# Filter groups of one batch each in a fused Fourier-filter and MLP-mixer kernel

## The chip, the cores and the metric

One core of one Trainium2 chip runs the whole program. The metric is the device time of one execution in microseconds, the median of the runs made. A separate, profiled execution supplies the trace. Engines are called as the profile calls them: PE is TensorE (PEld its weight loads), DVE is VectorE, ACT ScalarE, POOL GpSimd and SP SyncE, which issues most of the DMA transfers.

## The reference

All arrays are float32; x has 8 batches of 3008 tokens by 256 channels.

```python
X = np.fft.rfft(x, axis=1)                       # along the 3008 tokens
Y = X * (filt_r + 1j * filt_i)[None, :, :]       # 1505 frequencies x 256 channels
x = np.fft.irfft(Y, n=3008, axis=1)
h = np.maximum(x.transpose(0, 2, 1) @ w_tok1, 0.0) @ w_tok2     # 3008 -> 256 -> 3008
u = x + h.transpose(0, 2, 1)
out = u + np.maximum(u @ w_ch1, 0.0) @ w_ch2                    # 256 -> 1536 -> 256
```

## The kernel before, in words

**Two kinds of work share TensorE.** The *filter* (`dft`, L561) makes the Fourier transform, the product with the filter and most of the way back, for the batches of one group at a time (`GROUPS`, L56). The *mixer* (`mix`, L1132) does the two MLPs for one batch after another. The mixer is one long generator; after each piece of an item it yields a place, and the loop at L1319 decides there whether the next step of the filter of a coming group is issued. So the order of the work on every engine is written out by hand; nothing is scheduled later.

**The mixer's items.** A batch has six stretches of tokens, m = 0 to 5 (512 wide, the last 448), and each stretch six pairs of hidden blocks, jp = 0 to 5: 36 items a batch, numbered i within it. Products of matrices are done in seven parts by sums of operands in place of eight. In one item `up_first` makes four matmuls (L984), ACT copies one result away (L987), `up_middle` adds on VectorE (`hh<-ps_pg,s` and `s<-ps_pg,hh` at L962), `up_last` makes three matmuls (L1000) and its sums and ReLU, and `h_sums` and `down` work off the item before (L1018, seven matmuls). The places are 0 (behind the first part of `down`), 1 (behind `up_last`), 1.5 (behind the second part of `down`) and 2 (at the end). An fp32 matmul shows in the profile as two records, so L984 has eight records in an item. In each stretch `u_part` makes the operand of the next stretch: `u_quarter` in four parts for batches 1 to 7 (L905, L883), `u_unit` in two parts for batch 0 (L891, L883). `v_steps` and the six steps of `finish` (the residual sum and the transposes ahead of the output's stores) are VectorE work that `one_step` issues bit by bit. At item 32 (m = 5, jp = 2), place 2, `token_product` of the next batch runs: 12 rounds of 7 matmuls (L850), for which VectorE makes sums (`t4_sums`) and SP loads weights. The last six items of a batch are called its tail.

**The filter's steps.** Stage A is a transform of 64 points along one axis of the tokens, for a unit of 2 (untiled) or 4 (tiled) of its 24 columns. Stage B goes on along the other axis, multiplies with the filter and goes back, for 16 pairs of rows c. Between A and B, and behind B, the data goes through DRAM (`z_tmp`, `g_tmp`); the mixer loads the result as `t4`.
- Untiled stage A (`a_unit`, groups 0 and 1): 12 units a batch, each a full 128x128 matmul of 512 columns (L530), and a copy and a store (`z_out`).
- Tiled stage A (later groups): 6 units a batch. `x_sums` makes a sum and a difference of 512 columns on VectorE (L548, 0.68 us each), then `a_pair` makes four 64x64 matmuls on the four quarters of the array at once (L523). Such four are called a *set*. `leave` copies and stores.
- Stage B: `b_pair` is a set on what A left, `products` multiplies with the filter on VectorE (L705), `join` adds and subtracts (L710, L711), `bi_pair` is a set on the way back. In a group of two batches a set moves 512 columns, both batches beside each other, one c per step (`per = 1`). In a group of one batch `per = 2`: two c per step, two sets of 256 columns each for `b_pair` and for `bi_pair`.
- In tiled groups `bi_pair` of the step before follows directly on `b_pair`, so that one place on TensorE's order, here called a *slot*, has both. In group 1, which runs in batch 0, each has a place of its own.

**Where the groups stand.** Group 0 (batch 0) runs ahead of the mixer. Group 1 (batches 1 and 2) is issued within the mixer's batch 0, group 2 (3 and 4) in batches 1 and 2, group 3 (5 and 6) in batches 3 and 4, group 4 (batch 7) in batch 5; batches 6 and 7 carry none. A group must be done by item 32 of the last batch before its own; there the next group's generator starts and loads x. If it isn't, the build raises. Beside batch 0's first five items the last weights are converted as well (float64 bits to two float32 parts, on VectorE and ACT), and POOL makes the sums of w1, w2 and the channel weights in batch 0.

The table `due` (L1334 to L1343) names at which (jp, place) the coming step is issued. Its letters are the labels that `dft` yields: a (untiled unit), s (`x_sums`), d (two sets), c (`leave`), w (loads for B), b (`b_pair`), m (`join`), i (`bi_pair`).

Of the kernel before, what the change touches and what calls it, by code (L numbers as in the profile page):

```python
# [17 lines left out]
B = 8  # L18
# [37 lines left out]
GROUPS = ((0,), (1, 2), (3, 4), (5, 6), (7,))  # L56
# [71 lines left out]
def kernel(  # L128
# [432 lines left out]
    def dft(bs):  # L561
# [3 lines left out]
        per = 2 // nb if tiled else 1  # L565
# [40 lines left out]
        for i in range(0, len(todo) if tiled else 0, 2):  # L606
            if i + 2 == len(todo):
                zero_rows(0)
                w_load(0)
            sds = []  # L610
            for j in (i, i + 1):
                if j > i:
                    yield "s"
                sds.append(x_sums(*todo[j], j))
            yield "d"
            leave, leave_pg = [a_pair(*u, sd, tags) for u, sd, tags in zip(todo[i:i + 2], sds, (turn, ("pg", "pg")))]
            leave_pg()
            more(2)
            yield "c"
            leave()  # L620
            yield "s" if i + 2 < len(todo) else "w"
# [119 lines left out]
        if not first:  # L741
            last = K2 // KC
            for c in range(0, last, per):
                pss = b_pair(c)
                if c and tiled:
                    bi_pair(c - per, ("pg", "pg"))
                products(c, pss)
                for j in range(c + 2 * per, c + 3 * per):
                    if j < last:
                        t2_load(j)  # L750
                for j in range(c + min(2 * per, FB), c + min(2 * per, FB) + per):
                    if j < last:
                        w_load(j)
                yield "m"
                join(c)
                if not tiled or c + per == last:
                    yield "i"
                    bi_pair(c, turn)
                if c + per < last:
                    yield "b"  # L760
            return
# [79 lines left out]
    def token_product(b):  # L841
        one, two = (bank(tag).rearrange("p (s n) -> p s n", n=P) for tag in turn)
        for j in range(AP):
# [9 lines left out]
            if j + 2 < AP:  # L853
                t4_sums(b, j + 2)
        c = rp.tile([P, 8, P], FP32, tag="r", name="c")
# [276 lines left out]
    def mix(next_ready):  # L1132
# [11 lines left out]
        own = ({(4, 2): (0, 1)}, {(2, 2): (0,), (3, 0): (1,), (3, 2): (2, 3)})  # L1144
# [19 lines left out]
        for i in range(len(items) + 1):  # L1164
# [27 lines left out]
            if i < n:  # L1192
                one_step()
# [19 lines left out]
            if i >= n or i % n == n - 1:  # L1213
                one_step()
# [17 lines left out]
            if now:  # L1232
                if b + 1 < B and i % n == n - 4:
                    h1s[b + 1] = token_product(b + 1)
                u_parts(b, m, jp, 2)
                if jp == JP - 1:
                    while todo_v and m + 1 == MT:
                        one_step()
                if i >= 8 and to_dram:
                    to_dram.pop(0)()  # L1240
                if i in (28, 29):
                    w2m_load(i - 28)
# [5 lines left out]
    with tc.manual_schedule():  # L1248
# [70 lines left out]
        for b, i, place in mix(next_ready):  # L1319
# [10 lines left out]
            if done:  # L1330
# [4 lines left out]
            elif group:  # L1335
                tail = i >= n - JP
                sums_at = ((5, 1),) if tail else ((0, 1), (2, 1), (3, 1), (5, 1))
                due = (jp, place) in {"s": sums_at, "d": ((1, 1.5), (4, 1.5)), "c": ((2, 0), (5, 0)), "b": ((1, 1.5), (3 if tail else 4, 1.5)), "m": ((2, 2) if tail else (3, 1), (5, 1)),
                                      "i": ((0, 1.5), (3 if tail else 4, 1.5))}[coming]
            else:  # L1340
                due = (jp - (coming == "i")) % JP in ((5, 1, 2, 3) if i < 4 * JP else (5, 0, 1, 2, 3)) and place == {"b": 1, "m": 2, "i": 0}[coming]
            if coming == "a" and group == 0 and i < JP - 1:
                due = {0: 2, 1: 0, 1.5: 0, 2: 1}[place]  # L1343
# [34 lines left out]
```

## Time and profile before

| | |
|---|---|
| median of 3 runs | 2416.26 us (2415.17 to 2418.65) |
| profiled execution | 2418.01 us, span 2416.2 us |
| granted TensorE clock over the span | 0.996 |
| TensorE matmuls busy | 2374.1 us, 12340 records |
| VectorE busy | 1942.4 us |
| ScalarE, GpSimd busy | 690.5 us, 619.2 us |
| DMA | 278.65 MB, mean 115 GB/s |

How to read it: the span runs from the first to the last instruction of the program in the profiled execution, and that execution's own time is 1.8 us longer. "Busy" is the union of an engine's instructions. In a row of a group, the numbers behind the bar are busy time, mean duration of one, and idle time of the engine just before, with what ended it. In a row of a window they are listed in the order PE, PEld, DVE, ACT, POOL, then granted clock, DMA share and GB/s. The page's lines in 40 slices give the busy share in tenths.

### The profile page before, as it was taken

To read this page: it belongs to the slowest core of one execution; us is meant where nothing else is said; L and a number is where in the kernel's file an instruction comes from. 1 tells how busy PE (TensorE), PEld (TensorE's weight loads), DVE (VectorE), ACT (ScalarE), POOL (GpSimd) and SP (SyncE) were. 2 spreads that over 40 slices of the span, in tenths; PEclk is the share of its full clock that TensorE was granted. 3 is DMA by queue.
4 is the path that set the end of the run, shared out by engine and by line. 5 is a ranking of instruction groups with operands and counts; after the bars stand their busy time and mean duration, and the time that the engine had idled before them with its cause. 6 is when DMAs were issued, how large, how long until landed. Compare 5 with 4: busy or idle time off the path is not lost.

```text
span 2416.2 us, 35472 instructions
## 1 busy us (share of the span) xinstructions
PE 2374.1 (98%) x12340; PEld 1989.5 (82%) x12340; DVE 1942.4 (80%) x3673; ACT 690.5 (29%) x1339; POOL 619.2 (26%) x1115
## 2 busy tenths in 40 slices
PE   7989999999999999999999999999999999999998
PEld 4656676978888888988888888898888988898887
DVE  7798778777887888777788888877888777777776
ACT  5733322232222222123322222213222222222222
POOL 7476332113111211211121112112212112112121
PEclk8999999999999999999999999999999999999999
DMA  9985545534443223534344222344434111311100
GB/s 213 250 234 166 157 142 179 172 122 122 130 134 98 86 78 91 187 97 138 112 132 125 76 81 83 105 161 128 125 106 146 56 60 37 114 63 31 39 15 21
DMA packets 186011, 278.65 MB, mean 115 GB/s; under 512 B 35101, under 2 KB 122859, under 8 KB 185832
## 3 DMA queue, kind: packets, MB, share of 16 engines
q1 hardware_dynamic: 139544, 212.56, 28.7%
q0 software_dynamic: 34688, 53.83, 8.4%
q10 hardware_dynamic: 11600, 10.00, 1.4%
q8 instruction: 98, 1.61, 0.3%
q14 instruction: 81, 0.66, 0.1%
HBM read 193.52 MB, written 82.72 MB: 114 GB/s over the span
## 4 chain that ended last, share of the span: by engine, by line
PE 87%; DVE 6%; DMA 4%; issue 1%; POOL 1%; ACT 1%; SPq 0%; ACTq 0%; DVEq 0%; POOLq 0%
PE ps_po L1018 34%; PE ps_pg L984 19%; PE ps_pg L1000 14%; PE ps_b L523 4%; PE ps_b L850 3%; PE ps_acc L905 3%; PE ps_acc L850 2%; PE ps_b L905 2%; PE ps_pg L523 2%; PE ps_acc L883 2%; PE ps_b L883 2%; DMA st<-in_moe_w_tok_dram 1%; DVE t L962 1%; DVE hh L962 1%; DVE u L962 1%
## 5 line engine op out<-in xcount | busy, mean ns | idle before, releaser
L1026 POOL DMA_DIRECT2D out_dram<-r x752 | 407.9, 550 | 1611.9 <-issue 1149.2
L962 DVE TENSOR_TENSOR hh<-ps_pg,s 128x512 f32<-128x512 f32 (+3 forms) x864 | 482.4, 586 | 193.2 <-ACT s L987 191.3
L1005 ACT ACTIVATE hh<-hh 128x512 f32<-128x512 f32 (+1 forms) x576 | 347.8, 621 | 975.9 <-DVE hh L962 975.9
L1018 PE MATMUL ps_po<-t,wc 128*128 128x256 f32 (+1 forms) x2296 | 551.5, 379 | 1.8 <-DVE t L962 1.8
L1018 PEld LDWEIGHTS ps_po<-t,wc 128*128 128x128 f32 x2296 | 428.3, 190 | 110.2 <-issue 41.8
L984 PE MATMUL ps_pg<-v,wc 128*128 128x256 f32 (+1 forms) x1728 | 413.4, 376 | 1.7 <-POOL wc L381 1.6
L1018 PE MATMUL ps_po<-hh,wc 128*128 128x256 f32 (+1 forms) x1722 | 412.2, 375 | 0.6 <-POOL wc L382 0.6
L984 PEld LDWEIGHTS ps_pg<-v,wc 128*128 128x128 f32 x1728 | 327.9, 190 | 41.7 <-DVE v L962 3.2
L1018 PEld LDWEIGHTS ps_po<-hh,wc 128*128 128x128 f32 x1722 | 327.0, 190 | 39.4 <-POOL wc L382 1.7
L1000 PE MATMUL ps_pg<-u,wc 128*128 128x256 f32 (+1 forms) x1152 | 294.0, 378 | 1.9 <-DVE hh L962 1.3
L962 DVE TENSOR_TENSOR t<-t,hh 128x256 f32<-128x256 f32 (+1 forms) x576 | 246.2, 427 | 19.8
L1000 PEld LDWEIGHTS ps_pg<-u,wc 128*128 128x128 f32 x1152 | 216.3, 190 | 47.9 <-DVE hh L962 18.2
L962 DVE TENSOR_TENSOR s<-ps_pg,hh 128x512 f32<-128x512 f32 (+1 forms) x288 | 196.1, 681 | 30.7 <-DVE hh L962 0.9
L987 ACT COPY s<-ps_pg 128x256 f32<-128x256 f32 (+1 forms) x288 | 105.9, 368 | 343.6 <-PE ps_pg L984 339.3
L962 DVE TENSOR_TENSOR t<-hh 128x512 f32<-128x512 f32 (+1 forms) x288 | 195.4, 678 | 0.6 <-ACT hh L1005 0.6
L984 PE MATMUL ps_pg<-u,wc 128*128 128x256 f32 (+1 forms) x576 | 169.3, 376 | 2.4 <-DVE hh L962 2.4
L1000 PE MATMUL ps_pg<-v,wc 128*128 128x256 f32 (+1 forms) x576 | 168.9, 375 | 0.0
L984 PEld LDWEIGHTS ps_pg<-u,wc 128*128 128x128 f32 x576 | 108.3, 190 | 18.6 <-DVE hh L962 5.5
L1000 PEld LDWEIGHTS ps_pg<-v,wc 128*128 128x128 f32 x576 | 109.1, 190 | 12.7
L962 DVE TENSOR_TENSOR u<-ps_acc,u 128x256 f32<-128x256 f32 (+1 forms) x84 | 46.2, 550 | 80.4 <-PE ps_acc L905 56.9
L962 DVE TENSOR_TENSOR u<-ps_b,u 128x512 f32<-128x512 f32 (+2 forms) x126 | 74.5, 591 | 28.8 <-PE ps_b L905 26.7
L905 PE MATMUL ps_acc<-w 128*128 128x256 f32 (+1 forms) x336 | 85.3, 376 | 0.0
(164 smaller groups left out, 2638.6 us busy)
## 6 DMA issues: line engine op xcount, KB each, us to landing
w<-w_tmp SPq DMA_DIRECT2D x84, 448.0 KB
w<-w_tmp SPq DMA_DIRECT2D x35, 896.0 KB
out_dram<-r POOLq DMA_DIRECT2D x696, 32.0 KB, 2.2
g_tmp<-t SPq DMA_DIRECT2D x112, 192.0 KB
t<-g_tmp SPq DMA_DIRECT2D x42, 512.0 KB
t<-z_tmp SPq DMA_DIRECT2D x180, 96.0 KB
z_tmp<-t SPq DMA_DIRECT2D x60, 256.0 KB
filt<-in_x_dram SPq DMA_DIRECT2D x90, 128.0 KB
```

Source lines behind the costliest of these rows:

```text
L523: nc.tensor.matmul(outs(i, j), stat(i, j), mov(i, j), start=True, stop=True)
L850: nc.tensor.matmul(ps[:, at], w[:, n], mov, start=(j == 0 and i in (0, 2)), stop=(j == AP - 1 and i >= 5))
L883: nc.tensor.matmul(ps[:, ds(q * P, n)], t4[b, c][:, r, ts(dh, P)], wai[:, 0:n], start=(first and q == 0), stop=(not first and q == 3))
L905: nc.tensor.matmul(ps[:, ds(j * hw, hw)], h1[:, n, :], w2m[m % 2][:, at, 0:hw], start=(i < 2 and j == 0), stop=(j == len(todo) - 1))
L962: nc.vector.tensor_tensor(out=out, in0=in0, in1=in1, op=op)
L984: nc.tensor.matmul(ps[:, 0:hw], chan[0][:, jp, n, :], mov, start=True, stop=True)
L987: nc.scalar.copy(out=s[:, 0], in_=g[0][:, 0, 0:hw])
L1000: nc.tensor.matmul(ps[:, 0:hw], chan[0][:, jp, n, :], mov, start=True, stop=True)
L1005: nc.scalar.activation(out=hs, in_=hs, func=AF.Relu)
L1018: nc.tensor.matmul(po[i][:, j, 0:hw], chan[1][:, jp, n, :], mov, start=(jp == 0 and first == 1), stop=(jp == JP - 1 and last == 1))
L1026: q.dma_start(bass.AP(tensor=ob.tensor, offset=ob.offset + row * D + g * cw, ap=[[N1 * D, 32], [D if h else -D, n], [1, cw]]), blocks[ts(g ...
```

## The change

Each group now holds one batch, so there are eight groups, and batch b of the mixer carries the filter of batch b + 1, for b = 0 to 6. All groups but the first have `per = 2`: a slot of stage B has four sets of 256 columns in a row (two of `b_pair`, two of `bi_pair`), in batch 0 too. Group 1 (batch 1) keeps the untiled stage A, with half the units; batch 2 now goes through the tiled one.

The tiled stage A is laid out anew: a label e stands for one set alone. The first two units go as single sets in the tail of the batch before (jp 4 and 5), the other four as two double slots in m = 0. `x_sums` are issued one by one, and x is loaded one unit at a time behind each. The places of batch 0 become those of the other batches (stage B from item 6 on, two slots in each stretch), its untiled units come two per item instead of three, and its `u_unit` parts move to (3, 0) and (3, 2) from (4, 2). `token_product` becomes a generator that yields a place 1.7 in its tenth round, at which the table allows a `join` only. `one_step` is called in batch 0 where it is in the other batches.

```diff
-GROUPS = ((0,), (1, 2), (3, 4), (5, 6), (7,))
+GROUPS = tuple((b,) for b in range(B))
...
-        per = 2 // nb if tiled else 1
+        per = 1 if first else 2 // nb
...
-        for i in range(0, len(todo) if tiled else 0, 2):
-            if i + 2 == len(todo):
-                zero_rows(0)
-                w_load(0)
-            sds = []
-            for j in (i, i + 1):
-                if j > i:
-                    yield "s"
-                sds.append(x_sums(*todo[j], j))
-            yield "d"
-            leave, leave_pg = [a_pair(*u, sd, tags) for u, sd, tags in zip(todo[i:i + 2], sds, (turn, ("pg", "pg")))]
-            leave_pg()
-            more(2)
-            yield "c"
-            leave()
-            yield "s" if i + 2 < len(todo) else "w"
+        sums = []
+
+        def next_sum():
+            i = len(sums)
+            sums.append(x_sums(*todo[i], i))
+            more(1)
+
+        def sets(i, n):
+            return [a_pair(*u, sd, tags) for u, sd, tags in zip(todo[i:i + n], sums[i:], (turn, ("pg", "pg")))]
+
+        if tiled:
+            next_sum()
+            yield "s"
+            next_sum()
+            for i in range(2):
+                yield "e"
+                sets(i, 1)[0]()
+                yield "s"
+                next_sum()
+            for i in (2, 4):
+                yield "d"
+                leave, leave_pg = sets(i, 2)
+                leave_pg()
+                if i == 2:
+                    zero_rows(0)
+                    w_load(0)
+                yield "c"
+                leave()
+                for _ in range(2 * (i == 2)):
                     yield "s"
+                    next_sum()
+            yield "w"
...
-                if c and tiled:
+                if c:
                     bi_pair(c - per, ("pg", "pg"))
...
-                if not tiled or c + per == last:
+                if c + per == last:
                     yield "i"
                     bi_pair(c, turn)
...
             if j + 2 < AP:
                 t4_sums(b, j + 2)
+            if j + 3 == AP:
+                yield b - 1, MT * JP - 4, 1.7
...
-        own = ({(4, 2): (0, 1)}, {(2, 2): (0,), (3, 0): (1,), (3, 2): (2, 3)})
+        own = ({(3, 0): (0,), (3, 2): (1,)}, {(2, 2): (0,), (3, 0): (1,), (3, 2): (2, 3)})
...
-            if i < n:
+            if i < JP:
                 one_step()
...
-            if i >= n or i % n == n - 1:
+            if i >= JP:
                 one_step()
...
-                    h1s[b + 1] = token_product(b + 1)
+                    h1s[b + 1] = yield from token_product(b + 1)
...
-            if done:
+            if done or place == 1.7 and coming != "m":
                 continue
...
-            elif group:
+            else:
                 tail = i >= n - JP
-                sums_at = ((5, 1),) if tail else ((0, 1), (2, 1), (3, 1), (5, 1))
-                due = (jp, place) in {"s": sums_at, "d": ((1, 1.5), (4, 1.5)), "c": ((2, 0), (5, 0)), "b": ((1, 1.5), (3 if tail else 4, 1.5)), "m": ((2, 2) if tail else (3, 1), (5, 1)),
-                                      "i": ((0, 1.5), (3 if tail else 4, 1.5))}[coming]
-            else:
-                due = (jp - (coming == "i")) % JP in ((5, 1, 2, 3) if i < 4 * JP else (5, 0, 1, 2, 3)) and place == {"b": 1, "m": 2, "i": 0}[coming]
+                due = i >= JP * (group == 0) and (jp, place) in {
+                    "s": ((3, 1), (4, 1), (5, 1)) if tail else ((0, 1), (2, 1), (3, 1)),
+                    "e": ((4, 1.5), (5, 1.5)), "d": ((1, 1.5), (4, 1.5)), "c": ((2, 0), (5, 0)),
+                    "b": ((1, 1.5), (4, 1.5)), "m": ((2, 1.7) if tail else (3, 1), (5, 1)), "i": ((0, 1.5), (4, 1.5))}[coming]
             if coming == "a" and group == 0 and i < JP - 1:
-                due = {0: 2, 1: 0, 1.5: 0, 2: 1}[place]
+                due = place in (0, 2)
```

## Prediction

> **What bounds the kernel.** I read the page first (engines, clock, chain), then the windows of the eight batches, then TensorE's timeline item by item, then the windows of batch 0. From the page:
>
> ```profile
> PE 2374.1 (98%) x12340; PEld 1989.5 (82%) x12340; DVE 1942.4 (80%) x3673; ACT 690.5 (29%) x1339; POOL 619.2 (26%) x1115
> PEclk8999999999999999999999999999999999999999
> PE 87%; DVE 6%; DMA 4%; issue 1%; POOL 1%; ACT 1%; SPq 0%; ACTq 0%; DVEq 0%; POOLq 0%
> ```
>
> TensorE is busy 98% of the span at full granted clock, and 87% of the chain that ended last is its own. In the middle of the run a microsecond is won or lost only as TensorE work or as a gap in it. The windows below are cut at the first matmul (L984) of each batch:
>
> ```profile
> 139.40:476.60 337.20, 327.74 (x1614) 241.19 (x1613) 276.38 (x481) 99.99 (x191) 146.28 (x233) 1.00 0.57 173
> 476.60:764.60 288.00, 287.37 (x1541) 241.62 (x1540) 232.42 (x447) 80.10 (x158) 55.84 (x104) 1.00 0.40 125
> 764.60:1047.70 283.10, 283.10 (x1527) 242.00 (x1526) 235.72 (x443) 73.37 (x146) 54.38 (x101) 1.00 0.34 103
> 1047.70:1335.70 288.00, 287.36 (x1541) 241.60 (x1540) 232.41 (x447) 80.22 (x158) 55.80 (x104) 1.00 0.40 125
> 1335.70:1618.80 283.10, 283.10 (x1527) 241.98 (x1526) 235.69 (x443) 73.35 (x146) 54.37 (x101) 1.00 0.34 103
> 1618.80:1905.50 286.70, 285.96 (x1662) 246.11 (x1661) 234.72 (x461) 76.63 (x152) 55.92 (x104) 1.00 0.38 117
> 1905.50:2166.20 260.70, 260.70 (x1358) 237.09 (x1357) 199.22 (x401) 61.47 (x124) 54.36 (x101) 1.00 0.21 67
> ```
>
> After the bounds come the length and then the busy time of PE, PEld, DVE, ACT and POOL. Batch 6 carries no filter: 260.7 us is a bare batch. Batches 1 to 4 carry four filters for 27.3 + 22.4 + 27.3 + 22.4 us, batch 5 carries batch 7's alone for 26.0 us; together 125.4. Batch 0 carries two, beside the last weights, in 337.2 us. So the change takes one filter out of batch 0, gives one to batch 6, and recuts the ones between.
>
> **What a slot costs.** TensorE's timeline, an item with two sets of 512 columns and the bare item behind it, then one of batch 5 with four sets of 256:
>
> ```profile
> 1215.59 0.59 PE L984 MATMUL ps_pg<-u,wc 128*128 128x256 f32 x2
> ...
> 1221.77 1.04 PE L523 MATMUL ps_pg<-p,wb 64*64 64x512 f32 x8
> ...
> 1223.71 0.60 PE L984 MATMUL ps_pg<-u,wc 128*128 128x256 f32 x2
> ...
> 1229.75 0.60 PE L984 MATMUL ps_pg<-u,wc 128*128 128x256 f32 x2
> ```
> ```profile
> 1761.14 0.59 PE L984 MATMUL ps_pg<-u,wc 128*128 128x256 f32 x2
> ...
> 1767.33 1.04 PE L523 MATMUL ps_pg<-p,wb 64*64 64x256 f32 x16
> ...
> 1769.28 0.60 PE L984 MATMUL ps_pg<-u,wc 128*128 128x256 f32 x2
> ```
>
> From L984 to L984: 8.12 with the slot, 6.04 bare, so a slot of two 512 sets costs 2.08; four sets of 256 cost 8.14 - 6.04 = 2.10 (2.09 as a mean over batch 5). A slot with one 512 set or two 256 ones costs 1.22 (item of batch 1 at 620.1: 7.26). Hence 0.86 per 512 set and 0.36 per slot. The first slot of a batch's stage A (m0 jp1) costs more: 9.0 - 6.0 = 2.96, as the sums before it and the steps of `finish` push `up_middle` back on VectorE.
>
> [...]
>
> **Six tiled groups (batches 2 to 7), one batch each.** The places follow from the order of the yields and the `due` table.
> - Stage A: single sets in the last two items of the batch before (jp 4 and 5), at 1.22 each: 2.44. Then double ones at m0 jp1, with the sums at the same places as now: 2.96, and at jp4: 2.08.
> - Stage B: eight slots at jp1 and jp4 of m1 to m4. The first has only `b_pair`: 1.23. Seven with both: 7 x 2.09 = 14.63. The last `bi_pair` alone at m5 jp0: 6.89 - 5.67 = 1.22 by batch 2, plus 0.19 in the next item.
> - Sum 24.8 per group, 148.5 for six, against 125.4 now: **+23.1 us**.
>
> That counts the new `x_sums` in the tail at nothing. Each is two VectorE operations of 0.68. Their cover is VectorE's idle time there: in batch 2's tail it waits 1.27 and 1.55 us before `hh<-ps_pg,s` in the items at jp 4 and 5; the third sum lies where the present one does. 1.37 against 1.27 leaves about 0.1. Below, there is no gain to have from sums that are added. Above, the nearest row is the last `bi_pair` of batch 5, which in that tail cost 7.47 - 5.22 = 2.25 instead of 1.22 behind a joining of the same length: 1.0 per single set, 12 us over six tails. I take zero since the sums come after the operation that TensorE waits for next, while that joining came ahead of it.
>
> Edits with one answer. Products: four of 0.686 per slot in place of two of 1.217, 2.5 us more per batch on VectorE, which is at 235 of 283 us. Filter and table transfers for three more groups, on SP's queue ahead of w1, w2m and t4 loads: batch 5 issues exactly that many per batch at a DMA share of 0.38, without a gap in its slots of stage B. The t4 loads of a batch come in one go at the end, as they do in batches 2 and 4, whose token product takes 24.2 us as in batch 6. On SP's queue x units 3 to 5 and the z stores of the single sets now stand in the tail, ahead of the w2m load that m2 needs some nine items later. POOL's three clears of the filter rows (0.54 each) stand ahead of output stores that nobody waits for within a batch. The single sets' copies run on ACT, a quarter busy. In batch 0 the steps of `finish` move behind `up_last`, where later batches have them at bare items of 6.04. And the joining: the last one lies at m4 jp5, two items ahead of the token product, so at the new place nothing is waiting to be joined; that edit does nothing. Batch 5's late tail (7.47 above, and 24.46 for the product) goes for another reason, the earlier stage A, and is in the sum.
>
> **Batch 0, by rows of six items.** A full-array stage-A matmul is 0.85 us (two records). Windows of m0 and m2:
>
> ```profile
> 139.40:195.70 56.30, 49.79 (x182) 31.33 (x181) 50.46 (x89) 22.06 (x41) 45.39 (x75) 1.00 0.80 241
> 257.10:310.30 53.20, 52.48 (x257) 36.81 (x256) 44.34 (x74) 15.95 (x31) 18.78 (x31) 1.00 0.50 151
> ```
>
> - m0 (items 0 to 4 are the first row; 64.9 with item 5): VectorE, which still converts weights, is busy 50.5 of 56.3. Of 22 stage-A matmuls in batch 0 twelve go, five of them out of items 0 to 4; that frees TensorE, not VectorE. What helps is `u_unit`, 2.6 us each, now one at each of item 3's two places, not both at the end of item 4 (14.8 us). The sums of `v_steps` (1.5 us) move into this VectorE-bound stretch. I take 52 + 1.6 of waits for items 0 to 4 and 7.0 for item 5 (8.6 now): 60.5, or -4.5. Bounds: 0, if VectorE's queue stays as it is, and -9, by TensorE work alone.
> - m1 to m4 now: 52.8, 53.2, 52.2, 55.6. After: 6 x 6.04, two `u_unit` at 2.6, two slots of 2.09 = 45.7; m1 only 44.9, m4 0.4 less for its narrower `u`. I add 0.5 for waits (1.3 in m1, where POOL sums w1 and VectorE's 0.43 operations last 1.1): 46.2, 46.2, 46.2, 45.7, or -6.6, -7.0, -6.0, -9.9. Bounds: 1 us per row either way, the waits of now over the same count (52.2 - 51.2 in m3).
> - m5: `bi_pair` as in batch 2, 12.4 in place of 13.5: -1.1.
> - Sum **-35.1 us**.
>
> **Total.** 23.1 - 35.1 = -12.0. The profiled execution took 2418.0 (span 2416.2 and 1.8 around it), the median of the runs is 2416.3; 2416.3 - 12.0 = **2404**. One measurement can tell some 0.2% (4.8 us) from no change.
>
> **Rivals.**
> 1. The tail turns slower. Mechanism: VectorE's queue there. If x lands after the sum's place, or the sums run into `hh<-ps_pg,s`, `up_middle` waits and TensorE with it. For it: 1.37 us of work into 1.27 of idle time, twice in a row. Against: the first x transfer is issued at 1587.9 to 1590.9 in batch 4's tail, about 11 us ahead of the sum's place (1602.5). Price: the whole sums, 3 x 1.37 x 6 = 25 us, 2429. It decides from 16.8 / 6 = 2.8 us per tail on.
> 2. Batch 0 stays bound by VectorE and gives back little: m0 at 0 and 1 us less in each row, with 0.3 per tail: -2 to -5, 2411 to 2414. For it: 50.5 of 56.3 busy. Against: in m2 it is 44.3 of 53.2, and products and joins there fall from 15.3 to 8.3 us.
> 3. More is gained: the 0.88 us over a plain slot at m0 jp1 goes (6 x 0.88) and m0 saves 8: 2395.
> 4. That the change does not do what it says holds for the joining alone, as counted; if it did move, it would be a joining of 1.4 us beside the product's VectorE work, at most 1 us per tail.
>
> **Chances.** Forecast 0.64 (2398 to 2410), rival 1 0.10, rival 2 0.14, rival 3 0.12. Range 2396 to 2412: rival 1 and the far ends of 2 and 3 stay out. Faster by over 0.2% means below 2411.4: forecast, rival 3 and a third of rival 2, 0.80; within 0.2% 0.10; slower 0.10.
>
> **What would show it.** Batches 1 to 5 alike, each about 260.7 + 24.8 = 285.5 from L984 to L984; batch 6, without single sets in its tail, 283.1; batch 0 near 337.2 - 35.1 + 2.4 = 304.5, the 2.4 being the single sets in its tail, which the six groups' sum holds; batch 7 unchanged. Slots of m1 to m4 at 8.13. The tail's items at jp 4 and 5 1.2 us longer than now, 8.2 and 9.6. No joining (L710) between L850 records. Wrong if tail items grow by over 2 us, if items 0 to 4 of batch 0 stay at 56, or if slots of stage B show gaps.

## The result, and the profile after

The changed kernel takes 2410.6 us, the median of 9 runs (2407.8 to 2413.7); the kernel before took 2417.9 in the 9 runs beside them. The ratio is 0.9971, with a 95% interval of 0.9963 to 0.9979: 7.0 us less by the ratio (7.3 between the medians), where the prediction had 12.0. The profiled execution took 2411.5, with a span of 2409.7 against 2416.2. Line numbers below `zero_rows` (L588) moved down by 16 to 18: `up_first` is L1002 (was L984), `up_last` L1018 (was L1000), `down` L1036 (was L1018), VectorE's additions L980 (was L962), the joining L726, the products L721; `x_sums` stay at L548.

The page of the changed kernel, the same three lines:

```profile
PE 2363.4 (98%) x13132; PEld 2013.6 (84%) x13132; DVE 1954.8 (81%) x3781; ACT 689.2 (29%) x1339; POOL 629.8 (26%) x1124
PEclk8999999999999999999999999999999999999999
PE 91%; DVE 3%; DMA 2%; issue 1%; POOL 1%; ACT 1%; SPq 0%; DVEq 0%; ACTq 0%; POOLq 0%
```

TensorE has 792 more records in 10.7 us less busy time, and its share of the chain went from 87% to 91%, while VectorE's and the DMAs' shares were halved. The bound is the same. The clock's line in tenths shows nothing; the 6.8 us at half clock, shown below, are too short for a slice of 60 us. The windows of batches 0 to 6, cut at the weight load of their first L1002, 0.2 to 0.4 us ahead of the matmul itself (columns as before: length, PE, PEld, DVE, ACT, POOL, clock, DMA share, GB/s):

```profile
141.60:452.80 311.20, 296.81 (x1605) 240.79 (x1604) 253.50 (x472) 86.10 (x167) 147.28 (x233) 0.99 0.49 154
452.80:738.10 285.30, 285.29 (x1663) 245.98 (x1662) 234.83 (x461) 76.72 (x153) 56.78 (x104) 1.00 0.40 123
738.10:1022.90 284.80, 284.79 (x1662) 245.87 (x1661) 234.85 (x461) 76.68 (x153) 56.74 (x104) 1.00 0.40 124
...
1592.50:1877.50 285.00, 284.99 (x1661) 245.61 (x1660) 234.77 (x461) 76.38 (x153) 56.74 (x104) 1.00 0.40 123
1877.50:2159.90 282.40, 282.39 (x1646) 245.66 (x1646) 231.24 (x454) 74.84 (x149) 55.93 (x104) 1.00 0.36 112
```

Batches 1 to 5 are alike and filled to the last 0.01 us. The whole difference is found in four stretches of the span:

| stretch | before | forecast | after |
|---|---|---|---|
| start, up to batch 0 | 139.4 | 139.4 | 141.6 |
| batch 0 | 337.2 | 304.5 | 311.3 |
| batches 1 to 6 | 1689.6 | 1710.5 | 1707.0 |
| batch 7 | 250.1 | 250.1 | 249.8 |

The start has the same code in both kernels and took 137.8 to 142.2 in the twelve profiles of this study, so its 2.2 us lie within chance. Batches 1 to 6 cost 3.5 less than forecast. What is missing lies in batch 0, and there in one row of six items. Its m0, m1 and m2:

```profile
141.57:199.83 58.26, 50.20 (x200) 35.24 (x198) 55.04 (x99) 20.61 (x39) 46.56 (x76) 1.00 0.60 185
199.83:256.24 56.41, 50.09 (x243) 38.17 (x241) 42.44 (x66) 11.91 (x24) 35.55 (x48) 0.94 0.33 100
256.24:301.80 45.56, 45.56 (x257) 37.25 (x257) 36.73 (x69) 14.05 (x27) 18.43 (x31) 1.00 0.43 132
```

m2 is full and takes 45.6 (m3 and m4 45.7 each; forecast 46.2 and 45.7). m1 takes 56.4 where 46.2 was forecast: TensorE is idle for 6.3 of it, and the granted clock is 0.94. One item holds nearly all of that, item 7: 16.3 us. TensorE's timeline there, its releaser in brackets:

```profile
213.95 1.01 PE L523 MATMUL ps_acc<-t,wb 48*64 48x256 f32 x4
220.41 0.69 PE L523 MATMUL ps_b<-t,wb 48*64 48x256 f32 x2 [5.44 <-DMA t<-z_tmp]
```

The first slot of stage B has two sets of `b_pair`, each on a z unit of its own (the data that stage A left for one c). It ran the first and then stood 5.44 us for the second's z unit. The load was late because SP was late. SP's waits, its first instruction after the wait, and POOL's timeline at that time:

```profile
SPq L226 <- POOL filt L588: 40.4, 1, 40.4
```
```profile
206.53 0.31 SPq L226 DMA_DIRECT2D filt<-in_filt_r_dram  x1
...
209.77 0.30 SPq L667 DMA_DIRECT2D t<-z_tmp  x1
...
215.65 1.81 SPq L668 DMA_DIRECT2D t<-z_tmp  x4
```
```profile
199.26 6.78 POOL L829 TENSOR_TENSOR w<-w 128x384 f32<-128x384 f32 x6 [2.63 <-DMA w_tmp<-w]
205.98 1.45 POOL L588 MEMSET filt<- 128x512 f32 x3
207.40 11.13 POOL L829 TENSOR_TENSOR w<-w 128x384 f32<-128x384 f32 x10
```

Read from the bottom up: the three clears of the filter rows (`zero_rows`, L588) stand in POOL's queue behind six sums of w1 (L829). Those wait for the store of the raw w1 blocks and then take 6.8 us, so the first clear starts at 205.98. SP's queue holds the filter load, which overwrites the cleared tiles' other rows and waits for the clear, and behind it the z loads (L667, L668): those of the first unit from 209.77, then the next filter load, then those of the second unit from 215.65. The 40.4 us are SP's whole stand before that filter load, not a loss of that length. The clears need nothing of the sums; order alone puts them behind.

The kernel before had the same order, and its trace shows it too: POOL there runs all sixteen sums ahead of the clears, and the first set on a z unit comes 8.6 us after the first of them starts. POOL's timeline and TensorE's of the kernel before:

```profile
199.03 18.19 POOL L813 TENSOR_TENSOR w<-w 128x384 f32<-128x384 f32 x16 [4.27 <-DMA w_tmp<-w]
217.16 1.60 POOL L588 MEMSET filt<- 128x512 f32 x3
```
```profile
225.78 0.65 PE L523 MATMUL ps_b<-t,wb 48*64 48x512 f32 x2
...
234.73 0.65 PE L523 MATMUL ps_b<-t,wb 48*64 48x512 f32 x2
```

The change has the clears 11 us earlier and its first set 12.5 us earlier, at 213.24; that set still finds its z unit. But with `per = 2` the second set follows in the same slot, about 9 us after the clears start, where the kernel before has it in a later item, at 234.73, 17.6 us after them. So it is the second z unit that is no longer covered.

The idle time has a second price. The same row cut into stretches of 3.4 us, the seventh column the granted clock:

```profile
214.60:218.00 3.40, 0.37 (x2) 0.00 (x0) 3.40 (x5) 1.23 (x2) 3.16 (x4) 1.00 0.27 75
218.00:221.40 3.40, 0.99 (x8) 0.64 (x8) 1.08 (x1) 0.00 (x0) 0.53 (x1) 0.50 0.36 121
221.40:224.80 3.40, 3.40 (x13) 2.44 (x8) 2.48 (x4) 0.00 (x0) 0.00 (x0) 0.50 0.30 82
224.80:228.20 3.40, 3.40 (x17) 2.98 (x17) 2.23 (x5) 0.37 (x1) 0.00 (x0) 0.99 0.41 127
```

After a stretch in which TensorE was busy for 0.37 of 3.4 us the next one runs at half clock, and after one with 0.99 busy the next again. In the third stretch two records of L1002 take 1.06 us (223.69), at full clock 0.59 (556.99); by these rows I estimate half of 0.99 + 3.40, some 2.2 us more.

The tail of a batch answers the first rival. TensorE's timeline at the end of batch 2 (items of jp 4 and 5, each with a single set):

```profile
1013.49 0.54 PE L1002 MATMUL ps_pg<-u,wc 128*128 128x224 f32 x2
...
1021.20 0.65 PE L523 MATMUL ps_b<-sd,was 64*64 64x512 f32 x2
...
1023.08 0.59 PE L1002 MATMUL ps_pg<-u,wc 128*128 128x256 f32 x2
```

The item at jp 5 is 9.59 long, 8.38 before; that at jp 4 8.24, 7.02 before. Each is longer by 1.22, the bare price of a slot with one set, and VectorE still waits 1.58 us there after the new sum:

```profile
1012.02 1.28 DVE L548 TENSOR_TENSOR sd<-filt 128x512 f32<-128x512 f32 x2
1014.88 0.39 DVE L980 TENSOR_TENSOR hh<-ps_pg,s 128x224 f32<-128x224 f32 x1 [1.58 <-ACT s L1005]
```

### The profile page after: what moved, and what is told of

Same layout as the page of the kernel before. It is cut to its first block, busy times and chain, and to the rows that moved or that the text cites. A ratio compares the mean times of both kernels' runs of the same rounds, so it can differ in the third digit from the quotient of the medians.

```text
span 2409.7 us, 38162 instructions
## 1 busy us (share of the span) xinstructions
PE 2363.4 (98%) x13132; PEld 2013.6 (84%) x13132; DVE 1954.8 (81%) x3781; ACT 689.2 (29%) x1339; POOL 629.8 (26%) x1124
## 4 chain that ended last, share of the span: by engine, by line
PE 91%; DVE 3%; DMA 2%; issue 1%; POOL 1%; ACT 1%; SPq 0%; DVEq 0%; ACTq 0%; POOLq 0%
PE ps_po L1036 35%; PE ps_pg L1002 20%; PE ps_pg L1018 15%; PE ps_b L523 4%; PE ps_b L866 3%; PE ps_acc L923 3%; PE ps_acc L866 2%; PE ps_pg L523 2%; PE ps_b L923 2%; PE ps_b L901 2%; PE ps_acc L901 2%; DMA st<-in_moe_w_tok_dram 1%; DMA filt<-in_filt_r_dram 1%; DMA x<-in_x_dram 1%; DVE both L279 1%
## 5 line engine op out<-in xcount | busy, mean ns | idle before, releaser
L980 DVE TENSOR_TENSOR hh<-ps_pg,s 128x512 f32<-128x512 f32 (+3 forms) x864 | 481.4, 585 | 169.3 <-ACT s L1005 159.2
L1036 PE MATMUL ps_po<-t,wc 128*128 128x256 f32 (+1 forms) x2296 | 558.8, 380 | 0.5 <-DVE t L980 0.4
L1036 PEld LDWEIGHTS ps_po<-t,wc 128*128 128x128 f32 x2296 | 427.2, 190 | 96.4 <-issue 39.1
L1002 PE MATMUL ps_pg<-v,wc 128*128 128x256 f32 (+1 forms) x1728 | 412.7, 375 | 1.5 <-POOL wc L381 1.5
L1036 PE MATMUL ps_po<-hh,wc 128*128 128x256 f32 (+1 forms) x1722 | 411.5, 375 | 0.6 <-POOL wc L382 0.6
L1002 PEld LDWEIGHTS ps_pg<-v,wc 128*128 128x128 f32 x1728 | 328.2, 190 | 39.8 <-POOL wc L381 2.3
L1036 PEld LDWEIGHTS ps_po<-hh,wc 128*128 128x128 f32 x1722 | 326.8, 190 | 38.4 <-POOL wc L382 1.4
L1018 PE MATMUL ps_pg<-u,wc 128*128 128x256 f32 (+1 forms) x1152 | 291.9, 376 | 2.5 <-DVE hh L980 2.4
L980 DVE TENSOR_TENSOR t<-t,hh 128x256 f32<-128x256 f32 (+1 forms) x576 | 247.6, 430 | 19.8
L1018 PEld LDWEIGHTS ps_pg<-u,wc 128*128 128x128 f32 x1152 | 216.9, 190 | 34.1 <-DVE hh L980 8.0
L980 DVE TENSOR_TENSOR s<-ps_pg,hh 128x512 f32<-128x512 f32 (+1 forms) x288 | 196.0, 681 | 31.1 <-DVE hh L980 1.4
L980 DVE TENSOR_TENSOR t<-hh 128x512 f32<-128x512 f32 (+1 forms) x288 | 194.2, 674 | 0.6 <-ACT hh L1023 0.6
L1002 PE MATMUL ps_pg<-u,wc 128*128 128x256 f32 (+1 forms) x576 | 169.9, 377 | 3.9 <-DVE hh L980 3.9
L1018 PE MATMUL ps_pg<-v,wc 128*128 128x256 f32 (+1 forms) x576 | 168.8, 375 | 0.0
L1002 PEld LDWEIGHTS ps_pg<-u,wc 128*128 128x128 f32 x576 | 108.4, 191 | 20.1 <-DVE hh L980 7.8
L1018 PEld LDWEIGHTS ps_pg<-v,wc 128*128 128x128 f32 x576 | 108.9, 190 | 12.9
L980 DVE TENSOR_TENSOR u<-ps_acc,u 128x256 f32<-128x256 f32 (+1 forms) x84 | 46.1, 549 | 71.5 <-PE ps_acc L923 50.5
L980 DVE TENSOR_TENSOR u<-ps_b,u 128x512 f32<-128x512 f32 (+2 forms) x126 | 74.4, 591 | 28.9 <-PE ps_b L923 26.7
L721 DVE TENSOR_TENSOR p<-ps_b,filt 128x512 f32<-128x512 f32 x112 | 72.3, 685 | 16.2 <-PE ps_pg L523 13.4
```

The costliest lines, as they stand in the source:

```text
L721: nc.vector.tensor_tensor(out=prods[c, h][:, :, of(j)], in1=f, op=ALU.mult, in0=pss[h][:, of(j)].unsqueeze(1).to_broadcast([P, 2, nb, D]))
L980: nc.vector.tensor_tensor(out=out, in0=in0, in1=in1, op=op)
L1002: nc.tensor.matmul(ps[:, 0:hw], chan[0][:, jp, n, :], mov, start=True, stop=True)
L1018: nc.tensor.matmul(ps[:, 0:hw], chan[0][:, jp, n, :], mov, start=True, stop=True)
L1036: nc.tensor.matmul(po[i][:, j, 0:hw], chan[1][:, jp, n, :], mov, start=(jp == 0 and first == 1), stop=(jp == JP - 1 and last == 1))
```

## The experiments

Two questions were open: whether the wait in m1 comes from POOL's order, and what else of batch 0's rows each part of the change made. The table gives the rows of batch 0 in us (six items each; m5 takes 59.4 to 59.8 in all kernels of the changed layout), and the ratio to the kernel before. f2 and f4 are edits of the kernel before, all others of the changed one. The rows come from one profile each. e1 and e4 have the same code in batch 0, and their m1 takes 51.8 and 50.0; so a difference of that size in m1 is not told from chance. f3 leaves m0 and m1 as the changed kernel has them, and its item 7 takes 16.28 again.

| kernel | m0 | m1 | m2 | m3 | m4 | batch 0 | ratio (95%) |
|---|---|---|---|---|---|---|---|
| before | 64.9 | 52.8 | 53.2 | 52.2 | 55.6 | 337.2 | 1 |
| after | 58.3 | 56.4 | 45.6 | 45.7 | 45.7 | 311.3 | 0.9971 (0.9963 to 0.9979) |
| e1_early | 58.2 | 51.8 | 45.7 | 45.7 | 45.8 | 306.8 | 0.9954 (0.9939 to 0.9969) |
| e2_zero_dve | 59.5 | 48.4 | 45.7 | 45.7 | 45.8 | 304.7 | 0.9945 (0.9928 to 0.9961) |
| e3_early_u_late | 64.6 | 51.6 | 48.0 | 48.8 | 47.9 | 320.7 | 1.0003 (0.9994 to 1.0012) |
| e4_early_sum | 58.2 | 50.0 | 45.6 | 45.7 | 45.8 | 305.1 | 0.9963 (0.9948 to 0.9978) |
| f1_sums_later | 58.3 | 48.1 | 48.7 | 45.7 | 45.8 | 306.4 | 0.9948 (0.9935 to 0.9962) |
| f2_before_u_early | 67.1 | 54.9 | 53.1 | 53.1 | 55.8 | 341.6 | 1.0024 (1.0015 to 1.0034) |
| f3_tail_double | 58.1 | 56.2 | 45.7 | 45.7 | 45.8 | 310.9 | 0.9989 (0.9980 to 0.9998) |
| f4_before_sums_later | 64.9 | 56.4 | 53.9 | 52.2 | 55.2 | 341.0 | 1.0012 (1.0003 to 1.0021) |
| g1_sums_jp3 | 57.7 | 47.5 | 47.9 | 46.1 | 45.7 | 304.6 | 0.9949 (0.9935 to 0.9962) |
| g2_no_w1_sums | 58.1 | 45.2 | 45.7 | 45.7 | 45.7 | 299.9 | 2397.4 us, a single run |

**Group 1's last step, with the clears and loads, one item earlier** (`e1_early`):

```diff
-                due = place in (0, 2)
+                due = (place in (0, 2)) + ((i, place) == (JP - 2, 2))
```

> The step that clears the filter rows and issues batch 1's loads moves one item earlier, from item 5 (place 0) to the end of item 4, so that POOL gets the three clears ahead of the first six sums of w1. In the changed kernel item 7 of batch 0 takes 16.3 us, because the loads wait for the clears and these stand behind six sums that wait for a store. Theory (POOL's queue): the clears run at about 197 instead of 206, the loads follow, item 7 takes 7.3 to 8.5 us, and the whole is 8 to 9 us faster than the changed kernel, near 0.9936 of the kernel before (2402). Rival (the loads themselves, 27 transfers and the round trip through DRAM, are too slow for two items): item 7 stays over 13 us and the whole within 3 us of the changed kernel.

Medians 2406.9 against 2418.0. The z units are there in time (item 7 takes 7.9 in place of 16.3). POOL's timeline and the window of m1:

```profile
193.81 1.46 POOL L588 MEMSET filt<- 128x512 f32 x3
196.39 18.02 POOL L829 TENSOR_TENSOR w<-w 128x384 f32<-128x384 f32 x16 [1.11 <-DMA w_tmp<-w]
```
```profile
197.08:248.89 51.81, 48.41 (x241) 37.40 (x240) 41.06 (x66) 12.02 (x24) 34.16 (x45) 0.97 0.38 110
```

The clears now start 2.6 us ahead of the first sum, and 4.6 us of m1 come back; by the ratios the whole is about 4 us faster than the changed kernel, where 8 to 9 were expected. 6.6 above the row without the sums (45.2 in `g2_no_w1_sums`) stay: the wait for z is gone, but item 8 takes 10.89, with TensorE standing 2.66 us for VectorE at `up_last` and then 3.4 us at half clock. In e4's profile of the same code item 8 takes 9.43, and the clock is 1.00 from 205 to 232.

**The clears on VectorE** (`e2_zero_dve`):

```diff
-            nc.gpsimd.memset(filts[c][:, :, 0, :], 0.0)
+            (nc.vector if bs == GROUPS[1] else nc.gpsimd).memset(filts[c][:, :, 0, :], 0.0)
```

> Only the engine of the clears of group 1 changes, from POOL to VectorE; place and order of the loads stay as in the changed kernel. Theory (POOL's queue): the loads start when the last stage-A unit has left its buffer, near 196, and item 7 of batch 0 takes 7.5 to 9 us; item 5 grows by up to 1.5 us for three VectorE instructions; the whole is 6.5 to 8.5 us faster than the changed kernel. Rival (what the loads wait for is not the clears): item 7 stays at 16.

Medians 2403.2 against 2418.0. The clears leave POOL's queue and nothing else moves: m1 takes 48.4, 8.0 less, item 7 7.9. The window of m1, at full clock:

```profile
197.35:245.73 48.38, 46.12 (x239) 36.29 (x240) 39.71 (x66) 12.04 (x24) 32.31 (x44) 1.00 0.40 113
```

m0 pays 1.2 of it back (59.5), since VectorE, which sets the pace there, has the clears too (item 5: 7.44 in place of 5.97). e2 leaves the order of the loads alone, e1 leaves the engine alone, and both remove the wait; that it came from POOL's order is shown. By the ratios e2 is about 6 us faster than the changed kernel (6.5 to 8.5 expected).

**`u_unit` back at (4, 2)** (`e3_early_u_late`, on top of `e1_early`):

```diff
-        own = ({(3, 0): (0,), (3, 2): (1,)}, {(2, 2): (0,), (3, 0): (1,), (3, 2): (2, 3)})
+        own = ({(4, 2): (0, 1)}, {(2, 2): (0,), (3, 0): (1,), (3, 2): (2, 3)})
```

> As the kernel with the earlier loads, and the two u_unit parts of batch 0 go back to the end of jp 4, as before the change. Theory of the forecast: items 3 and 4 together grow by 2 to 3 us over the kernel with the earlier loads (in the changed kernel they take 13.2 + 9.0, before 10.4 + 14.8), since VectorE's conversions no longer lie under the first part; m1 to m4 stay within 0.3 us a row, where TensorE is the bound either way. Rival (the gain of m0 comes from the fewer stage-A matmuls): items 3 and 4 grow by less than 1 us.

Medians 2418.9 against 2418.0: all of the gain is gone, 12 us more than `e1_early`. m0 is back at 64.6 (before: 64.9), although five stage-A matmuls fewer lie in its first items: items 3 and 4 take 3.0 more than in `e1_early`, as the theory had it, and item 5, which it did not name, 3.5 more. And m2 to m4 take 2.1 to 3.1 us more, where 0.3 was expected: `u_unit` uses the banks of the slot just ahead. TensorE in m2, at jp 4:

```profile
290.58 1.13 PE L1036 MATMUL ps_po<-t,wc 128*128 128x256 f32 x4
293.37 1.95 PE L909 MATMUL ps_acc<-w,h 128*128 128x512 f32 x4 [1.66 <-DVE p L721]
```

The products (L721) of the slot at (4, 1.5) must have read `acc` before `u_unit` may write it. In the changed layout a slot lies at jp 4, so `u_unit` had to leave that place.

**The same move in the kernel before** (`f2_before_u_early`):

```diff
-        own = ({(4, 2): (0, 1)}, {(2, 2): (0,), (3, 0): (1,), (3, 2): (2, 3)})
+        own = ({(3, 0): (0,), (3, 2): (1,)}, {(2, 2): (0,), (3, 0): (1,), (3, 2): (2, 3)})
```

> The kernel before with one part of the change alone: batch 0's two u_unit parts at places (3, 0) and (3, 2). Theory (VectorE binds items 0 to 4, and the stand of u_unit matters elsewhere only where a slot's banks are in use): items 3 and 4 fall from 25.2 to about 22, m1 to m4 stay within 1 us a row; the whole is 1 to 4 us faster than the kernel before. Rival (moving u_unit frees TensorE in each row): all rows fall by 2 to 3 us, 10 us or more in the whole. Slower is possible too, if the steps at jp 3 then collide with the set at (3, 1): up to 2 us per row.

Medians 2424.2 against 2418.4: slower by 0.24%, where 1 to 4 us faster was expected. Items 3 and 4 fall from 25.2 to 22.8, near what was expected, but item 5 takes 13.8 in place of 8.6, and m0 67.1. There ACT stands 4.77 us in a copy of stage A for the store of an earlier one; the copy that `up_middle` needs is behind it in ACT's queue, TensorE then waits 3.24 us for `hh`, and the four records behind that wait take 1.63, where four of them take 1.03 in the kernel before (224.39):

```profile
198.41 0.58 ACT L539 COPY t<-ps_acc 128x512 f32<-128x512 f32 x1 [4.77 <-DMA z_tmp<-t]
200.32 1.63 PE L1000 MATMUL ps_pg<-u,wc 128*128 128x256 f32 x4 [3.24 <-DVE hh L962]
```

That alone is 5.2 us, more than batch 0 loses in all (4.5), so f2 does not price the move by itself. From m1 on the item at jp 3 takes 15.4, and the one at jp 4 gives most of that back (7.2, from 12.6). What e3 and f2 show is that here neither the new places without the move nor the move without the new places gained anything.

**The sums of w1 three items later** (`f1_sums_later`):

```diff
-            if JP - 2 <= i < JP + 2:
+            if i == JP - 2 or JP + 3 <= i < JP + 6:
```

> The changed kernel with POOL's sixteen sums of w1 issued in items 9 to 11 of batch 0 instead of items 5 to 7; nothing else moves. The clears of the filter rows then stand directly behind the channel weights' sums, and VectorE works beside an idle POOL in items 5 to 8. Theory (POOL does both harms in m1: its queue holds the loads back, and its own work slows VectorE's): item 6 6.1, item 7 7.3, item 8 6.1 to 7, items 9 to 11 up to 2 us more than in the changed kernel, m1 at 46 to 48 instead of 56.4, no half clock there; the whole 8 to 11 us faster than the changed kernel, near 0.993 of the kernel before. Rival (only the queue matters): as the kernel with the earlier loads, m1 at 51.8.

Medians 2407.1 against 2418.4; by the ratios between 5 and 6 us faster than the changed kernel, where 8 to 11 were expected. m1 comes out as the theory had it, not at the rival's 51.8. The wait goes here as well, by moving what stood ahead of the clears instead of the clears: item 7 takes 7.5. But the sums now slow items 10 to 13 (8.74, 8.42, 7.99, 9.25). Windows of m1 and m2:

```profile
199.86:248.01 48.15, 46.96 (x242) 36.62 (x240) 38.88 (x66) 12.01 (x24) 24.60 (x32) 1.00 0.33 94
248.01:296.73 48.72, 47.47 (x257) 36.82 (x257) 39.99 (x69) 13.93 (x27) 29.80 (x45) 1.00 0.47 148
```

**The same edit in the kernel before** (`f4_before_sums_later`):

> The kernel before with the sums of w1 in items 9 to 11, as a control: what the later sums bring without the change. There the loads of group 1 come two items later and the first set of stage B too, and items 5 to 8 are full of stage-A matmuls. Theory (the wait is made by the change): within 2 us of the kernel before. Rival (POOL's contention costs the kernel before as much): 5 us or more faster than it.

Medians 2421.2 against 2418.4: 2.8 slower, a little past the theory's 2, and nothing to be had; m1 rises by 3.6. In the kernel before, the late clears leave no wait that moving the sums could win back; the change took that cover away.

**The sums in two rounds of eight, at jp 3 of m1 and of m2** (`g1_sums_jp3`):

```diff
-            if JP - 2 <= i < JP + 2:
-                for _ in range(6 if i > JP - 2 else 1):
+            if i in (JP - 2, JP + 3, 2 * JP + 3):
+                for _ in range(8 if i > JP - 2 else 1):
...
-            elif i >= 2 * JP and i % 2 and w1_out:
+            elif i > 2 * JP + 3 and i % 2 and w1_out:
```

> The changed kernel with the sixteen sums of w1 in two lots of eight, in items 9 and 15 of batch 0, where u_unit gives TensorE 5.2 us more than VectorE's work there; the stores of the sums follow from item 17. Theory (the queue is free for the clears, and POOL's work lies where VectorE has room): items 5 to 8 as with the later sums (6.0, 6.0, 7.5, 6.0), items 10 to 13 lose most of the 5 us that the later sums cost there, m1 and m2 together 92 to 94 us (101.9 in the changed kernel, 96.8 with the sums in items 9 to 11); the whole near 2403 or below, 0.993 of the kernel before. Rival (VectorE is slowed wherever POOL works, and TensorE waits for it there too): m1 and m2 stay at 96 to 98.

Medians 2405.5 against 2417.4. m1 and m2 together take 95.4, f1's 96.9: between the theory's 92 to 94 and the rival's 96 to 98, and not clear of f1 by single profiles. Each round still costs: the items behind them take 8.74 and 7.81, then 8.79 and 7.54, where 8.03 and 6.04 are their lengths without sums.

**Without the sums** (`g2_no_w1_sums`):

```diff
-        for j in range(0, AP, 3):
+        for j in range(0, 0, 3):
```

> The changed kernel with the sixteen sums of w1 on POOL left out, so that the later token products work on unsummed weights. It bounds what POOL's work in m1 costs by queue and by contention together. Theory: the clears run at about 197, item 7 takes 7.3, m1 44.9 to 46 and m2 45.7, so 10.5 to 11.5 us less than in the changed kernel over the two rows. Rival (something else holds item 7): it stays over 12.

2397.4 in a single run. The windows of m0 and m1:

```profile
139.21:197.27 58.06, 51.45 (x200) 36.60 (x199) 54.85 (x99) 20.64 (x39) 47.18 (x78) 0.97 0.60 187
197.27:242.43 45.16, 45.16 (x241) 36.84 (x240) 35.76 (x67) 12.47 (x24) 16.30 (x27) 1.00 0.38 108
```

m1 is full, at 45.2: the prediction's count without waits was 44.9. So the forecast's items were sized rightly, and what m1 has above them goes with POOL's sums: first by their place ahead of the clears, as e1 and e2 show, and for the rest, by the rows on VectorE at the end of this document, by VectorE, which is slower beside them (2.24 us against 0.89 for two additions). In m0 the granted clock was 0.97, and the row is no longer for it: 58.06, against 58.26 at 1.00 in the changed kernel. TensorE does not set the pace there. m1 and m2 together take 90.8 here, and 94.0 to 97.5 with the sums in e1, e2, f1 and g1, wherever they stand.

**The first sum of m0 ahead of the first slot** (`e4_early_sum`, on top of `e1_early`):

```diff
-                    "s": ((3, 1), (4, 1), (5, 1)) if tail else ((0, 1), (2, 1), (3, 1)),
+                    "s": ((3, 1), (4, 1), (5, 1)) if tail else ((1, 0), (2, 1), (3, 1)),
```

> As the kernel with the earlier loads, and the fourth x_sums of each tiled group moves from item 0, place 1 to item 1, place 0, behind up_middle of item 1. In the changed kernel the slot of item 1 (m0 jp1) costs 2.64 us, 0.56 over a plain one. Theory (VectorE's order: these sums and the steps of finish push up_middle of item 1 back): the slot falls to 2.1 to 2.3, 0.3 to 0.5 us in each of six batches, 2 to 3 us in the whole. Rival (the finish steps alone hold VectorE, or the sums then come too late for the slot): no change, or worse by up to 0.7 us per batch.

Medians 2409.5 against 2418.0. The rival held: the item at m0 jp1 takes 9.15 in place of 8.65, in each of six batches: batches 1 to 6 rise from 1706.7 to 1709.6. (0, 1) is the better place of the two; why the first slot costs more than a plain one stays open.

**A double slot in the tail in place of two single ones** (`f3_tail_double`, its core):

```diff
-            for i in range(2):
-                yield "e"
-                sets(i, 1)[0]()
-                yield "s"
-                next_sum()
-            for i in (2, 4):
+            for i in (0, 2, 4):
...
-                for _ in range(2 * (i == 2)):
+                for _ in range(2 * (i < 4)):
...
-                    "s": ((3, 1), (4, 1), (5, 1)) if tail else ((0, 1), (2, 1), (3, 1)),
-                    "e": ((4, 1.5), (5, 1.5)), "d": ((1, 1.5), (4, 1.5)), "c": ((2, 0), (5, 0)),
+                    "s": ((3, 1), (4, 1)) if tail else ((0, 1), (0, 2), (2, 1), (3, 1)),
+                    "d": ((5, 1.5),) if tail else ((1, 1.5), (4, 1.5)), "c": ((0, 0), (2, 0), (5, 0)),
```

> The changed kernel with one double slot (jp 5, place 1.5) in the tail in place of two single sets; the third and fourth x_sums go to item 0, places 1 and 2. By the slot's fixed share of 0.36 us TensorE needs 0.36 less per batch, 2.2 us over six batches: the tail's items at jp 4 and 5 take 7.02 and 10.46 instead of 8.24 and 9.60. Against that VectorE has one more unit's sums (1.37 us) ahead of up_middle of item 1: theory (VectorE's queue decides at m0 jp1) the slot there rises from 2.64 to 3 to 4 us, and the whole is 0 to 6 us slower than the changed kernel. Rival (TensorE's work alone decides): 2 us faster.

Medians 2416.0 against 2418.4, by the ratios 4 to 5 us slower than the change, as the theory had it. The tail's two items do take less, 7.02 + 10.52 = 17.54 in place of 8.24 + 9.59 = 17.83: 0.29, near the 0.36 that a slot has fixed. But m0 now has the sums of two units ahead of its first slot, and there the first rival's mechanism works. VectorE and then TensorE in m0 of batch 3 (L975 and L1013 are L980 and L1018 of the changed kernel):

```profile
1029.70 1.28 DVE L548 TENSOR_TENSOR sd<-filt 128x512 f32<-128x512 f32 x2
1030.90 0.42 DVE L975 TENSOR_TENSOR hh<-ps_pg,s 128x256 f32<-128x256 f32 x1
```
```profile
1031.38 1.13 PE L1013 MATMUL ps_pg<-u,wc 128*128 128x256 f32 x4 [1.22 <-DVE hh L975]
```

`up_last` waits 1.22 us for an `hh` that stands behind the sum, and the item takes 9.87 in place of 8.66. With what the tail gains taken off, batches 1 to 6 are 5.5 us longer.

## Why the prediction was right, and what in it was wrong

The sign and the bound held: 2410.6 lies in the range of 2396 to 2412, near its upper end and 0.6 above the forecast's own 2398 to 2410. The mechanism held in the main: batch 0 gives 25.9, and batches 1 to 6 take 17.4 of it back. But that the time lies in the range is in part luck: the miss in m1 of batch 0 alone, 10.2 on 2404, would make 2414, outside it, and smaller errors the other way (steps 1, 5 and 7) brought it back. Step by step:

1. **Six tiled groups, +23.1.** Right in kind, 3.5 too high in batches 1 to 6. One full group costs 284.8 - 260.7 = 24.1, where 24.8 was forecast. Single sets in the tail 1.22 each, slots of stage B 8.13 - 6.04 = 2.09, the first 1.22, `bi_pair` at m5 jp0 1.22: as counted. The difference is m0: its first item takes 5.67, not 5.92, and the slot at jp1 costs 8.66 - 6.02 = 2.64, not 2.96.
2. **x_sums in the tail at nothing.** Right; the tail grew by the bare slots and by nothing else.
3. **Halved sets.** Right: the slots with four sets of 256 cost 2.09 in batches 1 to 6, where one with two sets of 512 costs 2.08 in the kernel before. So halving the sets costs about 0.01 us per slot here.
4. **The joining.** In batch 2 the last L726 is at 962.8, ahead of the token product at 975.6 to 999.8, and that item takes 24.22 as before. The edit does nothing, as counted.
5. **m0 of batch 0, -4.5.** It was -6.6, for the reason given: VectorE is busy 55.0 of 58.3, and e3 shows that the stage-A matmuls taken out, with all else that moved in m0, bring 0.3 without the move of `u_unit`. Items 0 to 4 take 52.3 (forecast 53.6), item 5 takes 5.97 (7.0).
6. **m1 of batch 0, -6.6.** This is the step that failed. It became +3.6: 10.2 us lie between forecast and result, twice the miss of the whole. When the z units of the first slot arrive is no term of the sum at all: their wait was put at nothing, without a reason. The one sentence on "POOL's three clears of the filter rows", which stand "ahead of output stores that nobody waits for", is among the tiled groups' edits, and it looked at what is behind the clears in POOL's queue. What is ahead of them decided in m1: six sums that wait for a store. And SP waits for the clears, with the z units that the slot needs behind that wait in its queue. And since `per = 2` asks for two units in one slot, the second came too late: TensorE stood 5.44 us, and the clock took an estimated 2.2 more. The rows of the kernel before that would have told it are shown above; I had read the length of the slots from the trace, but not when the operands of the first one come. The 1.3 that I had put into m1 for POOL's sums was the right suspect with a price for VectorE's slower operations alone.
7. **m2 to m5.** 45.6, 45.7, 45.7 against 46.2, 46.2, 45.7; there are no waits in them, and I had allowed 0.5. m5 has its 12.4 at jp 0 and 1.

Batch 0 came out 6.8 above the forecast: +10.2 in m1, -2.2 in m0, -1.2 in m2 to m4. With 3.5 less in batches 1 to 6, 2.2 of chance in the start and 0.3 less in batch 7, that takes the spans from the forecast's -11.8 to the -6.5 that was measured. The second rival named a time near the result (2411 to 2414), but not its cause: batch 0 gave the forecast's gain or more in every row but one, and that row was lost to a queue. Take the wait away, by e1, e2, f1 or g1, and batch 0 takes 304.6 to 306.8 (forecast 304.5), and the ratio is 0.9945 to 0.9954 (the forecast's 12.0 would be 0.9950). All four are faster than the kernel before. The intervals of e2, f1 and g1 lie just below that of the changed kernel, e1's overlaps it; among the four no order can be told. Without the sums of w1 (g2, a single run) batch 0 is another 4.7 to 6.9 us shorter; none of the places tried hides them.

What stays open: how much of the gain is the new cut of the groups and how much the new places in batch 0. e3 shows that the new places need `u_unit`'s move; the old stage-A layout with single-batch groups was not tried, since by the table its last set of stage B would come after the next group's start.

## What to carry to other kernels

When a step is moved, read each queue that it enters in both directions: what waits behind it, and what stands ahead of it and waits itself. Clears of 1.5 us on an engine that is busy for 26% of the span cost 8.0 us in m1 (by `e2_zero_dve`), because in POOL's queue they stood behind six sums that waited 2.63 us for another step's DMA and then took 6.78, and SP's queue passed that on to loads that had nothing to do with either. And a wait of TensorE in a full stretch can cost more than its length: here 5.44 us of idle time brought 6.8 us at half clock with them, by the estimate above 2.2 us more.

## What was not expected of the hardware

**The clock follows short waits.** In the changed kernel TensorE waits 5.44 us, until 220.41, and the granted clock is 0.50 from 218.0 to 224.8. In e1 a stretch with TensorE busy for 1.13 of 3.40 us is followed by one at half clock, in e3 one with 1.68 of 3.40:

```profile
240.90:244.30 3.40, 1.68 (x9) 0.97 (x6) 2.48 (x4) 1.07 (x2) 2.04 (x3) 0.99 0.54 155
244.30:247.70 3.40, 3.40 (x8) 1.78 (x7) 0.00 (x0) 0.00 (x0) 3.32 (x7) 0.50 0.72 228
```

The only idle time in that stretch of e3 is 1.72 us long; in e1 the idle time is 2.66 us. In both the half clock lasts 3.4 us, half of the 6.8 in the changed kernel, and the stretches here are cut to that length. With 1.74 of 3.40 us busy, in the same trace of e3, the clock stayed:

```profile
339.90:343.30 3.40, 1.74 (x7) 0.86 (x6) 2.20 (x4) 0.73 (x2) 1.98 (x4) 1.00 0.91 286
343.30:346.70 3.40, 3.40 (x16) 1.97 (x15) 0.00 (x0) 0.58 (x1) 3.32 (x7) 1.00 0.68 221
```

These rows give no sharp border: in e4 TensorE is busy for 1.64 of the 4.00 us from 216 to 220, and the clock is 1.00 there and up to 232. Which stretch of time counts for the clock, and from which share on, is not shown.

**VectorE beside POOL.** The same additions of `t<-t,hh`, first in the changed kernel while POOL sums w1, then in e2 after the sums:

```profile
212.09 2.24 DVE L980 TENSOR_TENSOR t<-t,hh 128x256 f32<-128x256 f32 x2
```
```profile
218.49 0.89 DVE L980 TENSOR_TENSOR t<-t,hh 128x256 f32<-128x256 f32 x2
```

2.24 against 0.89 for two of them. In the changed kernel the sums run until 218.5, in e2 they end at 213.1, ahead of the second row. The additions with a PSUM input (`hh<-ps_pg,s`) are not among those that stretch here: two of 128x512 take 1.28 beside the sums (214.26 in the changed kernel) and 1.28 after them (219.29 in e2). Why the others stretch is not shown.
